# Finding and spreading the largest row sum of a weight block on VectorE alone, and moving two narrowed tiles of x into block 4

## The chip, the cores and the metric

The kernel runs on one core of a Trainium2 chip. The core has TensorE (matrix products, written to PSUM), VectorE, ScalarE and GpSimd (elementwise work and reductions), and SP, from whose queue most DMA transfers are issued. Each engine works off its own queue in order and waits for the others by semaphores. The metric is the time of one execution on the device in microseconds, as the median of several runs; smaller is better.

## The reference, cut to what matters

Attention with the heads mixed before and after the softmax gives x, of 1792 tokens (4 batches of 448) and 768 features; behind it stands a gated layer:

```python
rms = np.sqrt(np.mean(x * x, axis=-1, keepdims=True) + 1e-06)
xn = x / rms * rms_g
g = xn @ w_gate                      # 768 x 1536
silu = g * (1.0 / (1.0 + np.exp(-g)))
val = xn @ w_val                     # 768 x 1536
return (silu * val @ w_out).astype(np.float32)   # 1536 x 768
```

The weights come in as float64. The change touches only the gated layer, and there only the way in which weights and x are brought into float16.

## The kernel before, in words

The program has three stages. Attention runs first, to about 360 us of the span. Then come the gate and value products, and last the product with w_out, in which seven products take the place of eight.

**The gate and value products.** The 1536 columns of `w_gate` and `w_val` are cut into 12 blocks `f` of 128 columns. For each block and each batch `b` (0 to 3) `product` (L648) makes two results in PSUM, `pg` and `pv`, each a sum over six tiles `kk` of 128 features, and for each of these three matmuls of 448 columns: high part of the weights by high part of x, high by low, low by high (L652 to L654). That is 18 matmuls for `pg`, 18 for `pv`, 144 in a block. `swiglu` (L678) then makes silu(pg) times pv on ScalarE and VectorE and combines the results of several batches and blocks on GpSimd (L697). PSUM has six buffers for pg and pv, so TensorE can be three batches ahead of `swiglu`.

**Two kinds of blocks.** Blocks 0 to 3 (`PLAIN = 4`) hold weights and x as pairs of float32 values with a shortened mantissa. Blocks 4 to 11 hold both as pairs of float16 values, `wh`, `wl` and `xn`. For that the 24 tiles of x (4 batches by six features' tiles) are narrowed while blocks 1 to 3 are computed: `x_narrow` (L889) is called 1, 1, 3 and 3 times behind the four batches of each. One call scales a tile on VectorE (L900), rounds it on ScalarE (L901) and subtracts on VectorE or, for every third tile, on GpSimd (L902); `x_fetch` asks for the next tile on SP's queue.

**Weights.** `queue` and `queue_out` write a list of half blocks to be fetched and converted; `fetch` keeps two transfers ahead, `convert` takes at most one half for each batch. A conversion is ScalarE's L541, four VectorE instructions (L516 to L519) and, for a float16 block, ScalarE's L554, which sums the absolute values of each row into `half.sums`, one column for each half. From block 4 on the halves of `w_out` stand in the list as well (`if f >= PLAIN`, L955).

**The scale of a float16 block.** `even(f + 1, stage)` (L864) makes a power of two from the largest row sum of the block, so that the float16 values fit. `spread_max` (L562) does this with TensorE: a float32 matmul with the unit matrix brings the two columns of 128 sums into two rows (L564), VectorE takes their maxima (L568), a second float32 matmul with a matrix of ones spreads the sum of both to all 128 partitions (L572), and `power` (L579) makes the scale and its inverse with four VectorE instructions (L581 to L584). Each of the two matmuls is two passes on TensorE. Then ScalarE writes `wh` (L877) and VectorE `wl` (L878), both halves behind each other. `gain` (L849) does the same once, in block 0, for the vector `rms_g`.

**Order.** The order of all queues is the order in which the code is written. In blocks 3 to 10 `even` is called around the products of batch 2 (stage 0 between pg and pv, stage 1 behind pv) and of batch 3 (stage 2 ahead of pg, stage 3 behind pv), before `convert`, `x_narrow` and `swiglu` of that batch. So L564 stands in TensorE's queue between pg and pv of batch 2, and L572 behind pv of batch 2.

Of the kernel before, what the change touches and what calls it, by code (L numbers as in the profile page):

```python
# [7 lines left out]
F32 = mybir.dt.float32  # L8
# [32 lines left out]
PLAIN = 4  # L41
LEAST, MOST = 2.0 ** -90, 2.0 ** 100
# [5 lines left out]
def attention_moe(ctx: ExitStack, tc, q, k, v, wpre, wpost, mask, ident, wgv, wo, rms_g, out):  # L48
# [473 lines left out]
    def load_w(src, kind, pool_name=None, plain=None):  # L522
# [9 lines left out]
        def half(p):  # L532
# [11 lines left out]
            if kind == "wide":  # L544
                ks = slice(KT * p, KT * p + KT)
                hi, lo = pair
                f = c.bitcast(F32).rearrange("p (a f) -> p a f", f=128)
                nc.scalar.activation(hi[:, ks], f, AF.Copy)
                nc.gpsimd.tensor_tensor(lo[:, ks], f, hi[:, ks].bitcast(F32), ALU.subtract)
            elif kind == "narrow":  # L550
                half.plain.append(c.bitcast(F32))
                if not p:
                    half.sums = b_pools["tiny"].tile([128, 2], F32, name="wsum", tag="wsum", bufs=2)
                nc.scalar.activation(narrow(pair)[0][:, KT * p : KT * p + KT], half.plain[p].rearrange("p (a f) -> p a f", f=128), AF.Abs, scale=2.0 ** -12, accum_out=half.sums[:, p : p + 1])  # L554
# [7 lines left out]
    def spread_max(cols, many):  # L562
        ps = b_pools["ps0"].tile([128, S], F32, name="pst", tag="pv")
        nc.tensor.matmul(ps[:many, :128], cols, eye, start=True, stop=True)  # L564

        def top():
            m = b_pools["tiny"].tile([2, 1], F32, name="top", tag="top", bufs=2)
            nc.vector.tensor_reduce(m[:many], ps[:many, :128], AX.X, ALU.max)  # L568

            def back():  # L570
                o = b_pools["ps0"].tile([128, S], F32, name="pst", tag="pv")
                nc.tensor.matmul(o[:, :1], ones[:many], m[:many], start=True, stop=True)  # L572
                return o[:, :1]

            return back

        return top

    def power(v, up, more, name):  # L579
        t, p, s_, inv = (b_pools["tiny"].tile([128, 1], I32 if i in (1, 2) else F32, name=f"{name}{i}", tag=f"{name}{i}", bufs=2) for i in range(4))  # L580
        nc.vector.tensor_scalar(t, v, LEAST, MOST, ALU.max, ALU.min)  # L581
        nc.vector.tensor_scalar(p, t.bitcast(I32), 23, 23, ALU.logical_shift_right, ALU.logical_shift_left)
        nc.vector.tensor_scalar(s_, p, -1.0, float((254 + up) * 2 ** 23), ALU.mult, ALU.add)
        nc.vector.tensor_scalar(inv, p.bitcast(F32), 2.0 ** -up, more, ALU.mult, ALU.mult)  # L584
        return s_.bitcast(F32), inv
# [201 lines left out]
    def part_b(ps_p):  # L787
# [61 lines left out]
        def gain(stage, held={}):  # L849
            if stage == 0:  # L850
                held["sum"] = b_pools["tiny"].tile([128, 1], F32, name="gsum")
                held["g"] = b_pools["tiny"].tile([128, KT], F32, name="gabs")
                nc.scalar.activation(held["g"], g_sb, AF.Abs, accum_out=held["sum"])
            elif stage == 1:
                held["top"] = spread_max(held["sum"], 1)
            elif stage == 2:
                held["back"] = held["top"]()
            elif stage == 3:
                v = held["back"]()
                up, held["down"] = power(v, 8, 1.0, "gain")  # L860
                nc.vector.tensor_scalar(held["g"], g_sb, up, None, ALU.mult)
            return held

        def even(f, stage, held={}):  # L864
            if stage == 0:
                held["top"] = spread_max(halves[f].sums, 2)
            elif stage == 1:
                held["back"] = held["top"]()
            elif stage == 2:
                held["v"] = held["back"]()  # L870
            else:
                up, unit[f] = power(held["v"], 2, gain(4)["down"], "unit")
                hi, lo = w[f] = narrow(halves[f].pair)
                for p, c in enumerate(halves[f].plain):
                    ks = slice(KT * p, KT * p + KT)
                    c = c.rearrange("p (a f) -> p a f", f=128)
                    nc.scalar.activation(hi[:, ks], c, AF.Copy, scale=up)  # L877
                    nc.vector.scalar_tensor_tensor(lo[:, ks], c, up, hi[:, ks], ALU.mult, ALU.subtract)  # L878
# [10 lines left out]
        def x_narrow(many):  # L889
            for i in range(min(many, len(loaded))):  # L890
# [9 lines left out]
                nc.vector.scalar_tensor_tensor(raw, raw, gain(4)["g"][:, kk : kk + 1], ry_ps[0], ALU.mult, ALU.mult)  # L900
# [3 lines left out]
        def first_row():  # L904
# [27 lines left out]
            gain(2)  # L932
# [3 lines left out]
            gain(3)  # L936
# [16 lines left out]
        for f in range(1, FT - 1):  # L953
            queue(f + 1)
            if f >= PLAIN and outs:  # L955
                queue_out(outs.pop(0), f)
        for f in range(1, FT):
            plain = f < PLAIN
            for b in range(B):
# [9 lines left out]
                if even_next and b == 3:  # L969
                    even(f + 1, 2)  # L970
# [6 lines left out]
                if even_next and b == 3:  # L977
# [142 lines left out]
```

## Time and profile before

| What | us |
|---|---|
| three runs | 861.67, 861.85, 865.72 |
| median | 861.85 |
| profiled execution | 865.68 |
| its span, first to last instruction | 863.9 |
| TensorE busy in the span | 826.2 (96%) |
| VectorE, ScalarE, GpSimd busy | 600.8, 420.7, 361.8 |

The profile is of one execution. Its rows give the start of an instruction from the span's start, its duration, and in brackets how long the engine stood idle before it and what ended that. Successive matmuls overlap: what one costs is the distance between starts, not its duration. "PE" is TensorE, "DVE" VectorE, "ACT" ScalarE, "POOL" GpSimd. Block f begins with its first matmul `pg`: block 1 at 387.21, block 4 at 481.65, block 5 at 510.68.

### The profile page before, as it was taken

To read this page: it belongs to the slowest core of one execution; us is meant where nothing else is said; L and a number is where in the kernel's file an instruction comes from. 1 tells how busy PE (TensorE), PEld (TensorE's weight loads), DVE (VectorE), ACT (ScalarE), POOL (GpSimd) and SP (SyncE) were. 2 spreads that over 40 slices of the span, in tenths; PEclk is the share of its full clock that TensorE was granted. 3 is DMA by queue.
4 is the path that set the end of the run, shared out by engine and by line. 5 is a ranking of instruction groups with operands and counts; after the bars stand their busy time and mean duration, and the time that the engine had idled before them with its cause. 6 is when DMAs were issued, how large, how long until landed. Compare 5 with 4: busy or idle time off the path is not lost. (4 is left out here: it accounts for less than half of the span.)

```text
span 863.9 us, 26658 instructions
## 1 busy us (share of the span) xinstructions
PE 826.2 (96%) x10936; PEld 615.1 (71%) x10936; DVE 600.8 (70%) x1055; ACT 420.7 (49%) x931; POOL 361.8 (42%) x497
## 2 busy tenths in 40 slices
PE   7899989899999998999998999999999999999998
PEld 2668777677777776799997645555555569999997
DVE  5687776688777766877777776668656249976561
ACT  3677766577767766743333333233332235553310
POOL 7233445364645457944644411212112158572210
PEclk9999999999999999999999999999999999999999
DMA  7787768666756653752565365655554246664531
GB/s 213 195 229 214 219 189 234 189 193 208 224 180 189 203 161 117 222 197 80 186 197 158 103 204 168 180 183 151 167 150 166 75 137 189 184 194 139 169 131 64
DMA packets 81020, 150.06 MB, mean 174 GB/s; under 512 B 10767, under 2 KB 70317, under 8 KB 80899
## 3 DMA queue, kind: packets, MB, share of 16 engines
q1 hardware_dynamic: 76286, 134.72, 51.7%
q0 software_dynamic: 3648, 11.31, 4.9%
q10 hardware_dynamic: 965, 2.34, 0.8%
q8 instruction: 86, 1.41, 0.7%
q14 instruction: 35, 0.29, 0.1%
HBM read 77.55 MB, written 31.21 MB: 126 GB/s over the span
## 5 line engine op out<-in xcount | busy, mean ns | idle before, releaser
L184 PE MATMUL sp<-r,wk_pre 64*64 64x448 f32 x720 | 167.4, 554 | 4.7 <-DMA r<-st 3.4
L136 PE MATMUL qk<-k,q 64*64 64x448 f32 x768 | 157.7, 572 | 6.0 <-DMA q<-in_q 4.2
L198 ACT ACTIVATE e<-sp,nm 128x448 f32<-128x448 f32 x180 | 114.4, 639 | 91.8 <-DVE nm L191 90.1
L191 DVE TENSOR_REDUCE nm<-sp 128x1 f32<-128x448 f32 x180 | 111.5, 623 | 58.0 <-PE qk L136 26.7
L225 PEld LDWEIGHTS pm<-wn,e 60*64 60x64 f32 x5152 | 111.5, 136 | 48.2 <-POOL wn L210 22.6
L225 PE MATMUL pm<-wn,e 60*64 60x60 f32 x5152 | 110.0, 222 | 15.1 <-issue 11.1
L210 POOL TENSOR_SCALAR wn<-wk,rp 128x60 f32<-128x60 f32 x180 | 55.8, 322 | 163.4 <-DVE rp L207 146.4
L697 POOL TENSOR_TENSOR keep<-sg,keep 128x448 f32<-128x448 f32 x24 | 29.9, 1247 | 170.3 <-DVE sg L691 112.7
L269 PE MATMUL av<-at_all,v 64*64 64x240 f32 (+4 forms) x1728 | 94.4, 321 | 2.2 <-issue 2.2
L184 PEld LDWEIGHTS sp<-r,wk_pre 64*64 64x64 f32 x720 | 63.1, 136 | 21.3 <-ACT e L198 9.0
L136 PEld LDWEIGHTS qk<-k,q 64*64 64x64 f32 x768 | 56.0, 138 | 28.4 <-issue 8.3
L269 PEld LDWEIGHTS av<-at_all,v 64*64 64x64 f32 x1728 | 71.1, 134 | 4.4 <-issue 3.9
L652 PE MATMUL pg<-xn,wh 128*128 128x448 f16 x192 | 67.8, 353 | 0.0
L652 PE MATMUL pv<-xn,wh 128*128 128x448 f16 x192 | 67.8, 353 | 0.0
L654 PE MATMUL pg<-xn,wl 128*128 128x448 f16 x192 | 67.7, 353 | 0.0
L653 PE MATMUL pg<-xn,wh 128*128 128x448 f16 x192 | 67.7, 353 | 0.0
L653 PE MATMUL pv<-xn,wh 128*128 128x448 f16 x192 | 67.7, 353 | 0.0
L654 PE MATMUL pv<-xn,wl 128*128 128x448 f16 x192 | 67.7, 353 | 0.0
L238 DVE COPY at_all<-pm 128x420 f32<-128x420 f32 x92 | 54.4, 591 | 16.6 <-PE pm L225 16.3
L639 DVE TENSOR_TENSOR h<-hraw,h 128x448 fp32r<-128x448 f32 x54 | 61.4, 1182 | 3.9 <-ACT h L638 3.9
L825 POOL TENSOR_TENSOR fac<-wo,fac 128x768 fp32r<-128x768 f32 x21 | 41.4, 1989 | 53.6 <-ACT fac L824 53.6
L652 PEld LDWEIGHTS <-wh 128*128 128x128 f16 x384 | 37.5, 98 | 35.6 <-issue 1.8
(161 smaller groups left out, 1861.2 us busy)
## 6 DMA issues: line engine op xcount, KB each, us to landing
r<-st SPq DMA_DIRECT2D x117, 210.0 KB
hraw<-td SPq DMA_DIRECT2D x84, 224.0 KB
wraw<-in_wgv SPq DMA_DIRECT2D x20, 768.0 KB
td<-keep SPq DMA_DIRECT2D x48, 224.0 KB
wraw<-in_wo SPq DMA_DIRECT2D x12, 768.0 KB
r<-st SPq DMA_DIRECT2D x44, 175.0 KB
v<-in_v SPq DMA_DIRECT2D x24, 256.0 KB
q<-in_q POOLq DMA_DIRECT2D x28, 192.0 KB, 6.0
```

The lines of the kernel that those rows point to most:

```text
L136: nc.tensor.matmul(ps[j][m, :S], qt[n][sl, hp, m], kt[n // NC, hp][sl], start=True, stop=True)
L184: nc.tensor.matmul(o, wk_pre[sl], rt[n][sl, 2 * p + v_], start=True, stop=True)
L191: nc.vector.tensor_reduce(t, ps[:, :S], AX.X, ALU.max, negate=True)
L198: nc.scalar.activation(e, ps[:, :S], AF.Exp, bias=nmx.pop((n, p, u)), accum_out=sm[n, p][:, u : u + 1])
L210: nc.gpsimd.tensor_scalar(wn[n, p][:, u], wk, r[:, u : u + 1], 1.0, ALU.mult, ALU.mult)
L225: nc.tensor.matmul(o[:, :, at_], e[u_][sl, j : j + JT], w_, start=True, stop=True)
L238: nc.vector.tensor_copy(dst, src)
L269: nc.tensor.matmul(x, vt[b, hp][sl, j, c_], a, start=(c_ == 0), stop=(c_ == JC - 1))
L639: nc.vector.tensor_tensor(lo, raw, hi.bitcast(F32), ALU.subtract)
L652: nc.tensor.matmul(ps, a, xh[:, kk], start=(kk == 0), stop=False)
L653: nc.tensor.matmul(ps, a, xl_[:, kk], start=False, stop=False)
L654: nc.tensor.matmul(ps, a2, xh[:, kk], start=False, stop=(kk == KT - 1))
```

## The change

Three things change.

1. `spread_max` is gone. `largest` takes its place, on VectorE alone: two copies fold the 128 partitions of the sums into 32 (64 onto 64, 32 onto 32, side by side), a reduction leaves one value in each of 32 partitions, a 32x32 transpose puts these into one row, a second reduction gives the largest, a `tensor_scalar` bounds it and writes it 32 times into a row, and a second transpose spreads it to 32 partitions. `power` computes on 32 partitions and copies the two results to 64 and then to 128. The largest sum of any row and half is taken, no longer the sum of two maxima.
2. `even` is now called once for each half, in batches 2 and 3 of blocks 3 to 10, behind the products of the batch: the first call does all of the scale and the first half of `wh` and `wl`, the second call the second half. `gain` has two stages in place of four.
3. `AT_ONCE` sets the calls of `x_narrow`: block 3 does 1, 1, 2 and 2 and block 4 does 1 and 1. The halves of `w_out` stand in the list from block 5 on.

```diff
+AT_ONCE = {1: (1, 1, 3, 3), 2: (1, 1, 3, 3), 3: (1, 1, 2, 2), 4: (1, 1, 0, 0)}
...
-    def spread_max(cols, many):
-        ps = b_pools["ps0"].tile([128, S], F32, name="pst", tag="pv")
-        nc.tensor.matmul(ps[:many, :128], cols, eye, start=True, stop=True)
...
+    def largest(b, many):
+        if "square" not in b_pools:
+            b_pools["square"] = b_pools["tiny"].tile([32, 2, 32], F32, name="square")
+            nc.vector.memset(b_pools["square"], 0.0)
+        z = b_pools["square"]
+        nc.vector.tensor_copy(b[:64, many : 2 * many], b[64:, :many])
+        nc.vector.tensor_copy(b[:32, 2 * many : 4 * many], b[32:64, : 2 * many])
+        nc.vector.tensor_reduce(z[:, 0, :1], b[:32, : 4 * many], AX.X, ALU.max)
+        nc.vector.transpose(z[:, 1], z[:, 0])
+        nc.vector.tensor_reduce(b[:1, :1], z[:1, 1], AX.X, ALU.max)
+        nc.vector.tensor_scalar(z[:1, 1], b[:1, :1].to_broadcast([1, 32]), LEAST, MOST, ALU.max, ALU.min)
+        nc.vector.transpose(z[:, 0], z[:, 1])
+        return z[:, 0, :1]
+
+    def power(t, up, more, name):
+        o = b_pools["tiny"].tile([128, 3], F32, name=name, tag=name, bufs=2)
+        p, s_, inv = (o[:, i : i + 1] for i in range(3))
+        q = [x[:32].bitcast(I32) for x in (p, s_)]
+        nc.vector.tensor_scalar(q[0], t.bitcast(I32), 23, 23, ALU.logical_shift_right, ALU.logical_shift_left)
+        nc.vector.tensor_scalar(q[1], q[0], -1.0, float((254 + up) * 2 ** 23), ALU.mult, ALU.add)
+        nc.vector.tensor_scalar(inv[:32], p[:32], 2.0 ** -up, more[:32] if more is not None else 1.0, ALU.mult, ALU.mult)
+        nc.vector.tensor_copy(o[32:64, 1:], o[:32, 1:])
+        nc.vector.tensor_copy(o[64:, 1:], o[:64, 1:])
+        return s_, inv
...
-            elif stage == 3:
-                v = held["back"]()
-                up, held["down"] = power(v, 8, 1.0, "gain")
+                up, held["down"] = power(largest(held["sum"], 1), 8, None, "gain")
...
+        def even(f, p, held={}):
+            half = halves[f]
+            if not p:
+                held["up"], unit[f] = power(largest(half.sums, 2), 2, gain(2)["down"], "unit")
+                w[f] = narrow(half.pair)
+            up = held["up"]
+            hi, lo = (t[:, KT * p : KT * p + KT] for t in w[f])
+            c = half.plain[p].rearrange("p (a f) -> p a f", f=128)
+            nc.scalar.activation(hi, c, AF.Copy, scale=up)
+            nc.vector.scalar_tensor_tensor(lo, c, up, hi, ALU.mult, ALU.subtract)
...
-            if f >= PLAIN and outs:
+            if f > PLAIN and outs:
...
                 product(pg, (hi[:, :KT], lo[:, :KT]), x)
-                if even_next and b == 2:
-                    even(f + 1, 0)
                 product(pv, (hi[:, KT:], lo[:, KT:]), x)
-                if even_next and b == 2:
-                    even(f + 1, 1)
-                if even_next and b == 3:
-                    even(f + 1, 3)
+                if even_next and b >= 2:
+                    even(f + 1, b - 2)
                 convert(f)
-                if plain:
-                    for _ in range((1, 1, 3, 3)[b]):
-                        x_narrow(1)
-                        x_fetch(3)
+                for _ in range(AT_ONCE[f][b] if f <= PLAIN else 0):
+                    x_narrow(1)
+                    x_fetch(3)
```

VectorE's queue in block 3, batch 2 and the start of batch 3, before. `top` holds the two maxima, `xs` and `xn` are tiles of x, `g` and `u` belong to `swiglu`, `wl` is the low half of the next block's weights (both halves, x2):

```order
L568 TENSOR_REDUCE top<-pst 2x1
L900 SCALAR_TENSOR_TENSOR xs<-xs,gabs,psn 128x448
L902 TENSOR_TENSOR xn<-xs,xn 128x448
L900 SCALAR_TENSOR_TENSOR xs<-xs,gabs,psn 128x448 x2
L902 TENSOR_TENSOR xn<-xs,xn 128x448
L685 TENSOR_TENSOR g<-pg,ry_7899 128x448
L687 TENSOR_TENSOR u<-pv,ry_7899 128x448
L581 TENSOR_SCALAR unit_8891<-pst 128x1
L582 TENSOR_SCALAR unit_8892<-unit_8891 128x1
L583 TENSOR_SCALAR unit_8893<-unit_8892 128x1
L584 TENSOR_SCALAR unit_8894<-unit_8892,gain_8084 128x1
L878 SCALAR_TENSOR_TENSOR wl<-wc,unit_8893,wh 128x768 x2
```

The same place now:

```order
L568 COPY wsum<-wsum 64x2
L569 COPY wsum<-wsum 32x4
L570 TENSOR_REDUCE square<-wsum 32x1
L571 STREAM_TRANSPOSE square<-square 32x32
L572 TENSOR_REDUCE wsum<-square 1x1
L573 TENSOR_SCALAR square<-wsum 1x32
L574 STREAM_TRANSPOSE square<-square 32x32
L581 TENSOR_SCALAR unit<-square 32x1
L582 TENSOR_SCALAR unit<-unit 32x1
L583 TENSOR_SCALAR unit<-unit,gain 32x1
L584 COPY unit<-unit 32x2
L585 COPY unit<-unit 64x2
```

The scale's instructions stand in one piece, ahead of the first tile of x. Behind these twelve rows stands the first half of `wl`, then two tiles of x and the g and u of batch 2, and only then the second half.

TensorE's queue in block 4, from the end of pg to the start of pv of batch 2, before (with the loads of weights between the matmuls; `pst` is the PSUM tile of the sums):

```order
L653 MATMUL pg<-xn,wh 128x448
L654 LDWEIGHTS wl
L654 MATMUL pg<-xn,wl 128x448
L564 MATMUL pst<-eye,wsum 2x128
L652 LDWEIGHTS wh
L652 MATMUL pv<-xn,wh 128x448
L653 LDWEIGHTS wh
L653 MATMUL pv<-xn,wh 128x448
```

The same place now:

```order
L654 MATMUL pg<-xn,wh 128x448
L655 LDWEIGHTS wl
L655 MATMUL pg<-xn,wl 128x448
L653 LDWEIGHTS wh
L653 MATMUL pv<-xn,wh 128x448
L654 LDWEIGHTS wh
L654 MATMUL pv<-xn,wh 128x448
```

The matmul into `pst` is gone, and pv follows pg without anything between them.

## Rows read from the trace of the kernel before

**Rows 1.** Windows by stage: us, busy us (instructions) by engine, clock, DMA share, GB/s.

```profile
360.00:500.00 140.00, 134.99 (x659) 114.23 (x657) 105.15 (x151) 53.16 (x90) 67.21 (x56) 0.99 0.51 164
...
528.00:556.00 28.00, 28.00 (x150) 14.30 (x148) 20.02 (x27) 9.12 (x14) 6.46 (x5) 1.00 0.67 193
```

**Rows 2.** Timeline of TensorE, steady blocks: start, us, engine, line, op, tiles.

```profile
510.68 0.35 PE L652 MATMUL pg<-xn,wh 128*128 128x448 f16 x1
...
527.51 0.35 PE L654 MATMUL pg<-xn,wl 128*128 128x448 f16 x1
...
528.11 0.36 PE L652 MATMUL pv<-xn,wh 128*128 128x448 f16 x1
...
555.58 0.35 PE L654 MATMUL pg<-xn,wl 128*128 128x448 f16 x1
```

**Rows 3.** Timeline of TensorE, block 3 and the start of block 4.

```profile
464.77 0.37 PE L654 MATMUL pg<-x,wl 128*128 128x448 f32 x1
...
468.19 0.38 PE L564 MATMUL pst<-eye,wsum 128*2 128x128 f32 x2 [3.06 <-ACT wh L554]
...
469.88 0.57 PE L652 MATMUL pv<-x,wh 128*128 128x448 f32 x1
...
473.23 0.37 PE L652 MATMUL pv<-x,wh 128*128 128x448 f32 x1
...
474.55 0.37 PE L653 MATMUL pg<-x,wh 128*128 128x448 f32 x1
...
481.65 0.36 PE L652 MATMUL pg<-xn,wh 128*128 128x448 f16 x1
```

**Rows 4.** Timeline of TensorE, block 4, first pair.

```profile
499.72 0.38 PE L564 MATMUL pst<-eye,wsum 128*2 128x128 f32 x2 [0.88 <-ACT wh L554]
```

**Rows 5.** Timeline of VectorE, blocks 1, 3 and 4.

```profile
387.59 0.77 DVE L352 TENSOR_SCALAR i<-var 112x4 int32<-112x4 int32 x1
...
469.71 0.62 DVE L687 TENSOR_TENSOR u<-pv,ry 128x448 f32<-128x448 f32 x1
...
477.16 0.15 DVE L582 TENSOR_SCALAR unit<-unit 128x1 int32<-128x1 int32 x1
477.35 0.15 DVE L583 TENSOR_SCALAR unit<-unit 128x1 int32<-128x1 int32 x1
...
478.51 1.95 DVE L878 SCALAR_TENSOR_TENSOR wl<-wc,unit,wh 128x768 f16<-128x768 f32 x2 [0.88 <-ACT wh L877]
...
480.38 0.68 DVE L900 SCALAR_TENSOR_TENSOR xs<-xs,gabs,psn 128x448 f32<-128x448 f32 x1
...
481.69 0.62 DVE L902 TENSOR_TENSOR xn<-xs,xn 128x448 f16<-128x448 f32 x1 [0.64 <-ACT xn L901]
...
485.57 0.61 DVE L687 TENSOR_TENSOR u<-pv,ry 128x448 f32<-128x448 f32 x1
...
500.22 0.68 DVE L691 SCALAR_TENSOR_TENSOR sg<-pv,unit,sg 128x448 f32<-128x448 f32 x1 [1.52 <-ACT sg L690]
500.82 0.27 DVE L568 TENSOR_REDUCE top<-pst 2x1 f32<-2x128 f32 x1
```

**Rows 6.** Timeline of GpSimd, blocks 1 and 3.

```profile
387.15 1.18 POOL L688 TENSOR_TENSOR keep<-sg,u 128x448 f32<-128x448 f32 x1
...
470.55 1.14 POOL L688 TENSOR_TENSOR sg<-sg,u 128x448 f32<-128x448 f32 x1 [6.37 <-DVE top L568]
...
474.37 1.15 POOL L697 TENSOR_TENSOR u<-sg,keep 128x448 f32<-128x448 f32 x1
...
477.29 1.15 POOL L688 TENSOR_TENSOR sg<-sg,u 128x448 f32<-128x448 f32 x1 [0.38 <-ACT sg L686]
```

**Rows 7.** Timeline of ScalarE, block 3.

```profile
477.54 0.94 ACT L877 ACTIVATE wh<-wc,unit 128x768 f16<-128x768 f32 x1 [0.33 <-DVE unit L583]
```

**Rows 8.** Timeline of block 0: TensorE, then VectorE.

```profile
378.69 0.47 PE L644 MATMUL pg<-x,wh 128*128 128x448 f32 x1
...
373.96 2.66 DVE L622 SCALAR_TENSOR_TENSOR x<-raw,g_sb,x 128x448 fp32r<-128x448 f32 x4 [2.42 <-ACT x L621]
```

More of the change, by code (lines that the diff above doesn't have):

```diff
@@ L552, in half @@
                 if not p:
-                    half.sums = b_pools["tiny"].tile([128, 2], F32, name="wsum", tag="wsum", bufs=2)
+                    half.sums = b_pools["tiny"].tile([128, 8], F32, name="wsum", tag="wsum", bufs=2)
                 nc.scalar.activation(narrow(pair)[0][:, KT * p : KT * p + KT], half.plain[p].rearrange("p (a f) -> p a f", f=128), AF.Abs, scale=2.0 ** -12, accum_out=half.sums[:, p : p + 1])
@@ L560, in narrow @@
         return [t.rearrange("p a f -> p (a f)").bitcast(F16)[:, : FT * 128].rearrange("p (a f) -> p a f", f=128) for t in pair]
-    def spread_max(cols, many):
-        ps = b_pools["ps0"].tile([128, S], F32, name="pst", tag="pv")
-        nc.tensor.matmul(ps[:many, :128], cols, eye, start=True, stop=True)
[L566 to L585, printed above, removed]
+    def largest(b, many):
[11 more added lines that the diff above has]
+        return z[:, 0, :1]
@@ L850, in gain @@
             if stage == 0:
-                held["sum"] = b_pools["tiny"].tile([128, 1], F32, name="gsum")
+                held["sum"] = b_pools["tiny"].tile([128, 4], F32, name="gsum")
                 held["g"] = b_pools["tiny"].tile([128, KT], F32, name="gabs")
-                nc.scalar.activation(held["g"], g_sb, AF.Abs, accum_out=held["sum"])
+                nc.scalar.activation(held["g"], g_sb, AF.Abs, accum_out=held["sum"][:, :1])
             elif stage == 1:
-                held["top"] = spread_max(held["sum"], 1)
-            elif stage == 2:
-                held["back"] = held["top"]()
-            elif stage == 3:
-                v = held["back"]()
-                up, held["down"] = power(v, 8, 1.0, "gain")
+                up, held["down"] = power(largest(held["sum"], 1), 8, None, "gain")
                 nc.vector.tensor_scalar(held["g"], g_sb, up, None, ALU.mult)
             return held
[L864 to L878, printed above, removed]
+        def even(f, p, held={}):
[8 more added lines that the diff above has]
+            nc.vector.scalar_tensor_tensor(lo, c, up, hi, ALU.mult, ALU.subtract)
         ahead_x = [(b, kk) for b in range(B) for kk in range(KT)]
@@ L899, in x_narrow @@
                 hi, lo = (t[:, kk] for t in xn[b])
-                nc.vector.scalar_tensor_tensor(raw, raw, gain(4)["g"][:, kk : kk + 1], ry_ps[0], ALU.mult, ALU.mult)
+                nc.vector.scalar_tensor_tensor(raw, raw, gain(2)["g"][:, kk : kk + 1], ry_ps[0], ALU.mult, ALU.mult)
                 nc.scalar.activation(hi, raw, AF.Copy)
@@ L931, in first_row @@
             convert(0)
-            gain(2)
             for kk in range(KT):
@@ L935, in first_row @@
             swiglu(2, 0, *first_ps[2])
-            gain(3)
             last_rms(0)
@@ L968, in part_b @@
                 even_next = PLAIN - 1 <= f < FT - 1
-                if even_next and b == 3:
-                    even(f + 1, 2)
                 product(pg, (hi[:, :KT], lo[:, :KT]), x)
-                if even_next and b == 2:
-                    even(f + 1, 0)
                 product(pv, (hi[:, KT:], lo[:, KT:]), x)
-                if even_next and b == 2:
-                    even(f + 1, 1)
-                if even_next and b == 3:
-                    even(f + 1, 3)
+                if even_next and b >= 2:
+                    even(f + 1, b - 2)
                 convert(f)
-                if plain:
-                    for _ in range((1, 1, 3, 3)[b]):
-                        x_narrow(1)
-                        x_fetch(3)
+                for _ in range(AT_ONCE[f][b] if f <= PLAIN else 0):
+                    x_narrow(1)
+                    x_fetch(3)
                 swiglu(b, f, pg, pv)
```

## The prediction, made before the result was known

> **What bounds the kernel now.** I read the windows by stage first, then TensorE's timeline, then the other engines at the places where TensorE waits. In blocks 4 to 11 of the gated product TensorE is busy without a hole: 28.00 of 28 us, while VectorE is busy 20.02 [rows 1]. The stretch of 360 to 500 us, blocks 0 to 3, is the only one behind the attention part in which it loses time: 134.99 of 140. So time can be won by taking instructions out of TensorE's queue, and by taking waits out of that queue; an idle VectorE in the steady blocks costs nothing.
>
> What the spreading of the largest row sum costs TensorE shows in its starts. In a steady block the last matmul of pg starts at 527.51 and the first of pv at 528.11, 0.60 us instead of one pitch. A pitch is 0.1891 us: 89 of them lie between the first matmul of the block, 510.68, and 527.51. From 527.51 to the same place a block later, 555.58, are 28.07 us, and 144 pitches are 27.23 [rows 2]. So the two pairs of float32 matmuls (L564 and L572) cost 0.84 us in a block.
>
> In block 3 they cost more, because there TensorE stands in its queue before a sum that is not there yet: the pair at 468.19 waited 3.06 us for ScalarE's L554, and behind that wait the pitch goes from 0.203 to 0.37 us between 469.88 and 473.23, nine matmuls at the lower of the clock's two levels, 1.2 instead of 2.4 GHz, that lose 1.5 us [rows 3]. From 464.77 to 474.55 are 9.78 us for 20 pitches of 0.203 (35 of them lie between 474.55 and 481.65): 5.7 us lost in block 3 [rows 3]. In block 4 the pair waits again, 0.88 us [rows 4]; with the 0.84 of the pairs themselves that is 1.7 us. In block 0 the gain has two such pairs, for which I take the same 0.84, 0.8 us.
>
> **The change part by part.** *The matmuls leave.* Eight spreadings and one gain leave TensorE's queue. On TensorE this is 0.8 (block 0) + 5.7 (block 3) + 1.7 (block 4) + 6 x 0.84 = 5.0 (blocks 5 to 10) = 13.2 us, all on the path, as no other engine makes TensorE wait there.
>
> *What VectorE gets.* A chain of 12 small instructions takes the place of five (L568, L581 to L584). Nearest rows: L582 starts at 477.16 and L583, which reads its result, at 477.35, so 0.19 us a step; 12 steps are 2.3 us. For the 32x32 transposes and the copies between partitions the trace has no row; from below 0.15 (the duration of L582), from above 0.27 (the reduction L568 over 128 elements) [rows 5]: 1.8 to 3.2 us. I take 0.19, since the new rows have at most 32 elements. The Trainium skill (VectorE: DVE Perf Modes, The three transpose paths) gives 311 ns for a 128x128 bf16 transpose on VectorE; by it, as an estimate, the chain would be 0.24 us longer, and no run here shows one.
>
> There is one more price in the trace. L352, on 112x4 elements in SBUF, took 0.77 us from 387.59, and ended at 388.36, just as GpSimd's L688 did (387.15 + 1.18); without such a neighbour L582 takes 0.15 [rows 5, 6]. But L583, on 128x1, ran its 0.15 us at 477.35 beside GpSimd's L688 of 477.29 [rows 5, 6]. So some small instructions wait out a GpSimd instruction and some do not. The Trainium skill (SBUF — State Buffer, SBUF: two separate sides) says that the port pair that VectorE and GpSimd share is locked for a whole instruction; the row of L352 agrees, L583 shows that not every small one asks for it. By the rule alone the sum would be that of the late bound below.
>
> In block 3 the chain stands right behind u of b=1, which ends at 470.33 [rows 5], and there GpSimd runs four instructions without a pause, 470.55 to 475.52 [rows 6]. With no wait the chain ends at 472.6; with a wait for each of three of them at 475.5. I take 474.4, two waits.
>
> *What is late next.* Behind the chain ScalarE writes the first half of wh and VectorE the first half of wl, 0.95 us each (L877 0.94, L878 1.95 for two) [rows 5, 7]: ready at 476.3. TensorE, freed of 0.8 + 5.7, would begin block 4 at 475.15 instead of 481.65 [rows 3]; it begins at about 475.9, as two matmuls come before the first of wl. The second half stands behind two tiles of x (0.67 each for L900, and once 0.64 of waiting and 0.63 of L902: 2.6), g, ScalarE's sg and wh, and its own 0.97: 481.9. TensorE wants it 18 x 0.189 = 3.4 us into the block, at 479.3, and effectively gets it at 481.5. So VectorE takes back 3.0 us in block 4's first tile.
>
> *The narrowed x.* Two of the last six tiles leave block 3 for block 4, one each behind its two conversions, (3,4) and (3,5). VectorE ended block 3's u at 486.18 before [rows 5]; with four tiles in place of six, the longer chain and ScalarE's two separate turns I get 486.8. In block 4 h of b=1 started at 500.22 [rows 5]; with that 0.6 and the two tiles (0.7 and 1.9) it starts at 503.0 to 503.4. TensorE uses (3,5) at the end of pg of b=3, within half a microsecond of its being ready: 0.4 us, held in the next sum. Behind h comes the chain for block 5, 2.3 us and, with one wait for GpSimd, 3.4, then ScalarE and VectorE 0.95 each: about 507.9, so TensorE begins block 5 at 507.5. Before it began at 510.68 [rows 2]. Of 0.8 + 5.7 + 1.7 = 8.2 us only 3.2 are left here; VectorE takes 5.0. With no port waits it begins at 505.1 (5.6 left), with the most of them at 508.8 (1.9 left).
>
> *The conversions of w_out* go a block later, blocks 5 to 10 instead of 4 to 9. That empties VectorE's queue in the second half of block 4, so it catches up by block 5; block 10 becomes like the others, and before, it had no such conversions. Their next use is in block 11 and behind: hidden, cost zero. If the cover were gone, one conversion of about 4 us would stand before the first factors. The fetches on SP keep their distance of two.
>
> *The gain chain*, a memset and 13 steps, now stands in block 0 ahead of a conversion. At 0.19 it puts VectorE back by 2.7 us, and by 3.8 with one wait for GpSimd. TensorE reads the tiles behind it (x of batch 3) from 378.69 on, and VectorE split them from 373.96 on, 0.67 us each, where TensorE takes 1.2 for each [rows 8]: 4.7 us of cover, less the 0.4 by which TensorE is early. Cost zero; without the cover, up to 3.8 us. Four of the old five steps and L568 leave VectorE later in the block.
>
> *From block 5 on* VectorE has 20.02 less 0.9 (the five old instructions) plus 2.3 to 5.5 and 1.9 of waiting for ScalarE, 23.3 to 26.5 us in a block of 27.27. It fits, so all of the 5.0 us stays.
>
> **Sum.** 3.2 + 5.0 = 8.2 us, bounds 6.9 (1.9 + 5.0) and 10.6 (5.6 + 5.0). The profiled execution took 865.68 us (span 863.9) and would take 857.5. The median of the three runs is 861.85, 3.8 lower; the stretch in question is behind the attention part, and I take the saving as the same there: 853.7 us.
>
> **The rivals.** (a) No port waits: 10.6 us, 851.3. For it: the waits are inferred from one row. Against: GpSimd is at work exactly then. (b) The new hole in block 4 lets TensorE's clock fall again, as 3.06 us did in block 3: 1.5 us more, 855.2. For it: 2.2 us idle at once; against: the 0.88 us in block 4 did nothing, and 2.2 lies between [rows 3, 4]. (c) VectorE takes nothing back, as its instructions pack closer than I laid them: 13.2 us, 848.7. (d) The freed matmul time becomes a wait of the same size, so that the blocks keep 28.07 us: 3.2 left, 858.6. For it: VectorE's sum of 26.5 is near 27.27. (e) Slower: the 12 steps each pay what L352 paid, 0.77 us, 9.2 in all. Then a steady block needs 20.0 - 0.9 + 9.2 + 1.9 = 30.2 us against 28.07, 2.1 x 6 = 13 us more, and blocks 3 and 4, whose chain is then 9.2 instead of 3.3 to 4.1 us, lose about 2.3 instead of winning 3.2: about 877. It decides from a chain of 7.1 us on. Against: GpSimd has at most four instructions in a row there. (f) That the new chain does not spread the number to all partitions would show in the order; the two copies at its end reach all 128, so I give it nothing.
>
> **How the numbers follow.** Forecast 0.40, (a) 0.20, (b) 0.15, (c) 0.08, (d) 0.12, (e) 0.05. The likeliest is 853.7. The range goes from just above (c) to just beyond (d), 849.2 to 858.8. A difference of 0.5%, 4.3 us, is about what can be told from no change, so faster means under 857.5: forecast, (a), (b) and (c) hold 0.83, less 0.05 because one of three runs lay 3.9 us above the others: 0.78. The same: 0.17. Slower: 0.05.
>
> **What would show it.** Right: no float32 matmul between pg and pv, a period of 27.2 to 27.4 us in blocks 5 to 10, and in block 4 a wait of pv for wl of about 2 us that stands where the 3.06 us stood. Wrong: holes of TensorE in the steady blocks, transposes of over 0.5 us, a block 5 that begins less than 1.9 us earlier than before (then the chain was under-priced), or copies that run freely beside GpSimd (then it was over-priced).

## The result, and the profile after

The changed kernel takes 857.98 us (median of 20 runs, 854.41 to 865.09); the kernel before, run beside it, took 865.57 (20 runs, 861.67 to 870.97). The ratio is 0.9917 with a 95% interval of 0.9895 to 0.9939: about 7 us faster, 5.3 to 9.1 by the interval. The prediction was 8.2 us faster and 853.7 us. The absolute time is 4.3 us off mainly because the kernel before, in these runs, was 3.7 us above the 861.85 from which the prediction counted.

The profiled execution of the changed kernel took 861.31 us, with a span of 859.4. These are the two windows of [rows 1] in it.

```profile
360.00:500.00 140.00, 134.23 (x655) 113.41 (x654) 108.29 (x161) 51.22 (x88) 67.02 (x57) 0.99 0.49 153
528.00:556.00 28.00, 28.00 (x150) 14.48 (x149) 21.39 (x36) 9.14 (x14) 6.05 (x6) 1.00 0.63 185
```

In the steady window VectorE does 21.39 us where it did 20.02, and TensorE is still without a hole. Between 360 and 500 us TensorE is no fuller than it was, 134.23 against 134.99. So I looked for the gain in the steady blocks first, and TensorE's timeline says how much it is. It answers [rows 2]: the last matmul of a pg and the first of the next pv, and the first of block 7 and of block 8.

```profile
565.61 0.35 PE L653 MATMUL pg<-xn,wh 128*128 128x448 f16 x1
...
568.82 0.35 PE L655 MATMUL pg<-xn,wl 128*128 128x448 f16 x1
569.01 0.35 PE L653 MATMUL pv<-xn,wh 128*128 128x448 f16 x1
...
592.85 0.35 PE L653 MATMUL pg<-xn,wh 128*128 128x448 f16 x1
```

From 568.82 to 569.01 is one pitch, and from 565.61 to 592.85 are 27.24 us in place of 28.07. The float32 matmuls are gone, and each of blocks 6 to 10 has its 0.83 us back. The same stretch that [rows 3] shows, the end of block 3 and what follows, now reads so on TensorE:

```profile
478.89 0.55 PE L653 MATMUL pg<-xn,wh 128*128 128x448 f16 x1 [3.35 <-ACT wh L868]
...
479.94 0.56 PE L655 MATMUL pg<-xn,wl 128*128 128x448 f16 x1
...
482.16 0.41 PE L655 MATMUL pg<-xn,wl 128*128 128x448 f16 x1
482.40 0.35 PE L653 MATMUL pg<-xn,wh 128*128 128x448 f16 x1
...
486.02 0.36 PE L655 MATMUL pv<-xn,wl 128*128 128x448 f16 x1 [1.05 <-DVE wl L869]
...
510.44 0.36 PE L653 MATMUL pg<-xn,wh 128*128 128x448 f16 x1 [0.79 <-ACT wh L868]
...
511.49 0.36 PE L655 MATMUL pg<-xn,wl 128*128 128x448 f16 x1 [0.50 <-DVE wl L869]
```

The 3.06 us of waiting inside block 3 have become 3.35 us at the start of block 4, with 1.05 more at its first pv and 0.79 and 0.50 at the start of block 5. From 479.94 to 482.16 the pitch is 0.35 to 0.37 us, the lower of the clock's two levels, until it comes back to 0.19 at 482.40.

To compare executions I count from the first matmul of batch 1 in block 0, called the start of the stage here, since the attention part before it ends some us earlier or later in each execution. These are the first and the last matmul of it, before and then after:

```profile
363.52 0.72 PE L644 MATMUL pg<-x,wh 128*128 128x448 f32 x1
...
859.69 0.37 PE L654 MATMUL po<-h,fac 128*128 128x448 f32 x1
```

```profile
364.07 0.72 PE L645 MATMUL pg<-x,wh 128*128 128x448 f32 x1
...
855.22 0.37 PE L655 MATMUL po<-h,fac 128*128 128x448 f32 x1
```

From start to start the stage takes 496.17 and 491.15 us, 5.0 less. Block 5 starts 147.16 us into the stage before and 146.37 after. So blocks 0 to 4 brought 0.8 us where 3.2 were forecast, and the rest 4.2: six times 0.83, less the 0.7 us that block 5 still waits inside itself. That is the gap to explain. The medians differ by 7.6 us; the 2.6 beyond the stage's 5.0 lie outside the stage or in the scatter, and I don't explain them.

A stage time is that of one execution, and it scatters too. Up to block 5 the kernels `chain_x3` and `chain_x5` below are the changed kernel, instruction for instruction: block 5 starts 147.37 and 146.09 us into the stage there, against 146.37 here. So a difference of 1.3 us between two stages, or less, shows nothing by itself.

Next VectorE's row in block 3: u, the chain (L568 to L585) and the two halves of wl.

```profile
472.27 0.61 DVE L688 TENSOR_TENSOR u<-pv,ry 128x448 f32<-128x448 f32 x1
472.92 0.17 DVE L568 COPY wsum<-wsum 64x2 f32<-64x2 f32 x1
473.12 1.17 DVE L569 COPY wsum<-wsum 32x4 f32<-32x4 f32 x1
474.32 0.15 DVE L570 TENSOR_REDUCE square<-wsum 32x1 f32<-32x8 f32 x1
474.50 0.20 DVE L571 STREAM_TRANSPOSE square<-square 32x32 f32<-32x32 f32 x1
...
474.95 0.58 DVE L573 TENSOR_SCALAR square<-wsum 1x32 f32<-1x32 f32 x1
...
475.79 0.14 DVE L581 TENSOR_SCALAR unit<-square 32x1 int32<-32x1 int32 x1
...
476.26 0.45 DVE L584 COPY unit<-unit 32x2 f32<-32x2 f32 x1
476.75 1.05 DVE L585 COPY unit<-unit 64x2 f32<-64x2 f32 x1
478.87 1.02 DVE L869 SCALAR_TENSOR_TENSOR wl<-wc,unit,wh 128x768 f16<-128x768 f32 x1 [1.06 <-ACT wh L868]
...
484.40 1.57 DVE L869 SCALAR_TENSOR_TENSOR wl<-wc,unit,wh 128x768 f16<-128x768 f32 x1 [1.00 <-ACT wh L868]
```

And beside it GpSimd, the same four instructions as in [rows 6]:

```profile
473.11 1.16 POOL L689 TENSOR_TENSOR sg<-sg,u 128x448 f32<-128x448 f32 x1 [6.38 <-DVE wsum L568]
474.35 1.15 POOL L698 TENSOR_TENSOR keep<-sg,keep 128x448 f32<-128x448 f32 x1
475.57 1.13 POOL L698 TENSOR_TENSOR keep<-keep 128x448 f32<-128x448 f32 x1
476.66 1.13 POOL L698 TENSOR_TENSOR u<-sg,keep 128x448 f32<-128x448 f32 x1
```

The chain takes 4.9 us, 472.92 to 477.80. Its long rows end where a GpSimd row ends: L569 at 474.29 (GpSimd 474.27), L573 at 475.53 (475.50), L584 at 476.71 (476.70), L585 at 477.80 (477.79). Reductions, transposes and operations on one element a partition take 0.14 to 0.20 in the midst of it.

And in block 0, where the prediction gave the gain chain no cost:

```profile
368.43 0.15 DVE L568 COPY gsum<-gsum 64x1 f32<-64x1 f32 x1 [1.35 <-ACT gabs L854]
368.62 0.85 DVE L569 COPY gsum<-gsum 32x2 f32<-32x2 f32 x1
...
371.50 0.55 DVE L517 TENSOR_SCALAR wc<-wc 128x768 f32<-128x768 f32 x1
```

The same conversion before:

```profile
368.27 0.70 DVE L516 TENSOR_SCALAR wc<-wc 128x768 f32<-128x768 f32 x1 [2.16 <-ACT wc L541]
```

It starts 7.43 us into the stage now and started 4.75 us in before, so it is 2.7 us late, the forecast number. By u of batch 2 in block 0 2.0 us of that are left (23.56 us into the stage for 21.53). VectorE waits nowhere for TensorE between there and block 3, and these 2.0 stay: u of batch 1 in block 3 stands at 108.20 and stood at 106.19 [rows 5].

### The profile page after: what moved, and what is told of

Read it like the earlier page. It is cut to its first block, busy times and chain, and to the rows that moved or that the text cites. A ratio compares the mean times of both kernels' runs of the same rounds, so it can differ in the third digit from the quotient of the medians.

```text
span 859.4 us, 26654 instructions
## 1 busy us (share of the span) xinstructions
PE 814.8 (95%) x10900; PEld 608.2 (71%) x10900; DVE 615.8 (72%) x1119; ACT 422.0 (49%) x931; POOL 360.3 (42%) x497
## 3 DMA queue, kind: packets, MB, share of 16 engines
q8 instruction: 86, 1.41, 0.7%
## 5 line engine op out<-in xcount | busy, mean ns | idle before, releaser
L185 PE MATMUL sp<-r,wk_pre 64*64 64x448 f32 x720 | 162.2, 540 | 5.2 <-DMA r<-st 1.8
L137 PE MATMUL qk<-k,q 64*64 64x448 f32 x768 | 153.3, 556 | 6.3 <-DMA q<-in_q 4.1
L655 PEld LDWEIGHTS <-wl 128*128 128x128 f16 x384 | 37.7, 98 | 38.4 <-DVE wl L869 3.3
```

Of the source, the lines that this page charges most:

```text
L137: nc.tensor.matmul(ps[j][m, :S], qt[n][sl, hp, m], kt[n // NC, hp][sl], start=True, stop=True)
L185: nc.tensor.matmul(o, wk_pre[sl], rt[n][sl, 2 * p + v_], start=True, stop=True)
L655: nc.tensor.matmul(ps, a2, xh[:, kk], start=False, stop=(kk == KT - 1))
```

## The experiments

Two theories stood against each other. **A**: VectorE's row of work from block 0 to the chain for block 5 sets when TensorE can go on in blocks 4 and 5, and the gain was lost there, 2.0 us by the gain chain and the rest by copies that wait out GpSimd. **B**: the loss sits on TensorE itself, in a clock that falls behind a wait or in waits that the moved tiles or conversions bring.

### The two halves of the change

`x_and_wo_only` is the kernel before with only the new places of x and w_out:

```diff
+AT_ONCE = {1: (1, 1, 3, 3), 2: (1, 1, 3, 3), 3: (1, 1, 2, 2), 4: (1, 1, 0, 0)}
...
-            if f >= PLAIN and outs:
+            if f > PLAIN and outs:
...
-                    for _ in range((1, 1, 3, 3)[b]):
+                for _ in range(AT_ONCE[f][b] if f <= PLAIN else 0):
```

> The kernel before with the moved tiles of x and the later w_out conversions alone; the sums still go through TensorE. My theory (the gain is TensorE's float32 matmuls and the wait in front of them): L564 still waits about 3 us in block 3, since the two conversions ahead of its sum are unmoved, the steady period stays 28.07 us, and the time is within 2 us of before. Rival (the moved tiles bring the gain, by emptying VectorE in block 3): 4 to 7 us faster than before, with a block 3 of under 33 us.

Measured: 864.31 us, ratio 0.9988 (0.9956 to 1.002); the stage takes 496.86 us, and the period, the time from one steady block to the next, is 28.07. The waits of TensorE between 400 and 690 us (what waited, for what: us in all, times, longest) are now one, where there were two:

```profile
PE pst L565 <- ACT wh L555: 3.6, 1, 3.6
```

`spread_only` is the other half, the new chain with the old places:

```diff
-AT_ONCE = {1: (1, 1, 3, 3), 2: (1, 1, 3, 3), 3: (1, 1, 2, 2), 4: (1, 1, 0, 0)}
+AT_ONCE = {1: (1, 1, 3, 3), 2: (1, 1, 3, 3), 3: (1, 1, 3, 3), 4: (0, 0, 0, 0)}
...
-            if f > PLAIN and outs:
+            if f >= PLAIN and outs:
```

> The changed kernel with x and w_out as before; only the sums are on VectorE. My theory: the steady period is 27.24 us all the same, and VectorE, with one more tile of x (1.3 to 1.9 us) ahead of the second half of wl in block 3 and conversions of w_out right behind the chain in block 4, delays blocks 4 and 5: 1 to 3 us slower than the changed kernel, still 3 to 6 us faster than before. Rival (the moved tiles bring the gain): as slow as before.

Measured: 860.78 us, ratio 0.9965 (0.9937 to 0.9992); the stage takes 494.12 us, period 27.24. So the steady blocks win their 0.83 us by the chain alone, and the moved tiles and conversions bring nothing alone but 3.0 us (494.12 to 491.15) once the chain stands on VectorE: the tile takes work out of the row in front of block 4's second half of wl. What the tiles bring and what the conversions was not run apart. The waits of pv in block 4 were 1.79 and 0.65 us here, and the clock fell a second time.

### What makes VectorE late

`gain_by_tensor` is the changed kernel with the gain's largest sum found as before, by two float32 matmuls, a reduction and four small steps:

```diff
-                up, held["down"] = power(largest(held["sum"], 1), 8, None, "gain")
+                nc.tensor.matmul(ps[:1, :128], held["sum"][:, :1], eye, start=True, stop=True)
...
+                nc.tensor.matmul(o[:, :1], ones[:1], held["top"][:1], start=True, stop=True)
```

> The changed kernel, but the gain of block 0 still goes through TensorE; the eight scales of the blocks are on VectorE. Theory A (the gain chain put VectorE back by 2.7 us in block 0, and 2.0 of it stayed until block 3, because VectorE waits for nothing of TensorE in between): u of batch 1 in block 3 comes 2.0 us earlier against the start of the stage, TensorE waits 1.3 instead of 3.35 us at the start of block 4, its clock does not fall behind it (1.5 us more), and the time is 2 to 3 us shorter than the changed kernel's, the 0.8 us of the two pairs already taken off. Theory B (VectorE was late in this one profile by chance): the wait in block 4 stays between 2 and 3.5 us and the time is 0.8 us longer than the changed kernel's.

Measured: 857.39 us, ratio 0.9927 (0.9896 to 0.9958). u of batch 1 in block 3 (u of block 3, from here on) stands 106.55 us into the stage, so 1.6 of the 2.0 us of delay are gone. That is more than the scatter: the four executions with the gain's chain of copies on VectorE have it at 107.90 to 109.22 (`chain_x5` 107.90, `spread_only` 108.09, 108.20 after the change, `chain_x3` 109.22), the three with the gain on TensorE (before, `x_and_wo_only` and this one) at 106.19 to 106.69. Block 4 starts after a wait of 0.44 us instead of 3.35; 1.3 of the difference is that TensorE comes later itself, with its float32 pairs of block 0 back (block 3 starts 83.02 us into the stage instead of 81.72). The clock doesn't fall, and the stage takes 489.49 us, 1.7 less than after the change. The times of whole runs can't tell 1.7 us.

`reduce_copies` leaves the chain where it is, but its four copies and the broadcast become reductions over an axis of one element, which compute the same:

```diff
+    def copy(o, x):
+        nc.vector.tensor_reduce(o, x.unsqueeze(2), AX.X, ALU.max)
...
-        nc.vector.tensor_copy(b[:64, many : 2 * many], b[64:, :many])
+        copy(b[:64, many : 2 * many], b[64:, :many])
...
-        nc.vector.tensor_scalar(z[:1, 1], b[:1, :1].to_broadcast([1, 32]), LEAST, MOST, ALU.max, ALU.min)
+        nc.vector.tensor_scalar(b[:1, 1:2], b[:1, :1], LEAST, MOST, ALU.max, ALU.min)
+        copy(z[:1, 1], b[:1, 1:2].to_broadcast([1, 32]))
...
```

> The changed kernel, but the four small copies and the instruction that writes the bounded maximum 32 times are reductions over an axis of one element, which the profile never showed waiting for GpSimd; one small instruction more. Theory A (the copies wait out GpSimd's instructions): the chain of block 3 takes 2.4 to 2.7 us instead of 4.9, whatever GpSimd does, TensorE waits about 1 us instead of 3.35 at the start of block 4, and the time is 2.4 to 4 us shorter than the changed kernel's (the larger if the clock does not fall). Theory B (the long copies are slow for another reason, their crossing of partitions): the chain stays at 4 to 5 us and the time is the changed kernel's.

Measured: 854.43 us, ratio 0.9896 (0.9854 to 0.9939), and the stage takes 487.02 us, 4.1 less than after the change. VectorE's row in block 3 (two copies, the broadcast, two copies), then GpSimd's beside it:

```profile
469.89 0.33 DVE L564 TENSOR_REDUCE wsum<-wsum 64x2 f32<-64x2 f32 x2
...
471.05 0.17 DVE L564 TENSOR_REDUCE square<-wsum 1x32 f32<-1x32 f32 x1
...
471.96 0.33 DVE L564 TENSOR_REDUCE unit<-unit 32x2 f32<-32x2 f32 x2
```

```profile
470.08 1.15 POOL L693 TENSOR_TENSOR sg<-sg,u 128x448 f32<-128x448 f32 x1 [6.38 <-DVE wsum L564]
471.30 1.15 POOL L702 TENSOR_TENSOR keep<-sg,keep 128x448 f32<-128x448 f32 x1
```

Thirteen instructions take 2.4 us in the midst of the same GpSimd work, 0.33 for each pair of former copies, where one copy took up to 1.17. The data and the engine are the same, the kind of instruction is another: so it was the kind that waited. The Trainium skill (SBUF — State Buffer, SBUF: two separate sides) says more than the prediction quoted: VectorE asks for the port pair that it shares with GpSimd in a perf mode that uses two ports, or with two inputs from SBUF. These rows agree with that as far as they go: copies and a tensor_scalar over several elements waited, reductions didn't. In which mode an instruction ran no row shows.

### Do the two delays add up, and what is left

`both_mends` has both edits.

> The changed kernel with both mends at once: the gain's largest sum by TensorE as before the change, and the chain's four copies and its broadcast as reductions over an axis of one element. By theory A (the gain chain made VectorE late in block 0; the copies wait out GpSimd's instructions) the two losses lie one behind the other on VectorE, so u of the second tile of block 3 comes 106.0 to 106.6 us behind the stage's first matmul (gain by TensorE alone 106.55, reductions alone 107.20) and the chain takes 2.4 us; but TensorE pays about 0.8 again in block 0. The stage lasts about 486.9 us (reductions alone 487.02). Rival B: the two mend the same delay, since with reductions the gain chain has no waits left to lose; then u comes at 107.2 and the stage is 0.8 us longer than with the reductions alone, 487.8.

Measured: 854.74 us, ratio 0.9882 (0.9844 to 0.9920); u of block 3 at 106.23 us, the stage 485.99. That is where theory A has u, and the stage is 1.8 us under rival B's 487.8. Against the reductions alone it is 1.0 us, which two executions of one program can differ by, so that the two delays add up is likely and not shown by the stage alone. What TensorE still waits between 400 and 690 us:

```profile
PE pv L659 <- DVE wl L890: 1.1, 1, 1.1
PE pg L659 <- DVE wl L890: 0.5, 1, 0.5
```

`early_half` starts from `reduce_copies` and asks whether the waits of pv in block 4 are a loss of their own:

```diff
-                    even(f + 1, b - 2)
+                    if f > PLAIN:
+                        even(f + 1, b - 2)
+                    elif b == 2:
+                        even(f + 1, 0)
+                        even(f + 1, 1)
```

> The kernel with reductions in place of the copies, and in blocks 3 and 4 both halves of the next block's weights are made right behind the chain, the second no longer behind the tiles of x of the tile between. With reductions alone pv of block 4 still waits 1.27 us for wh and 1.04 for wl, and pg of block 5 0.25 and 0.50. Theory C: what VectorE has to do between the chain of block 3 and the chain of block 4 sets when block 5 can begin, so the 2.3 us that pv no longer waits come back as a longer wait at the start of block 5 (3.0 us in place of 0.75), and the stage stays within 0.5 us of 487.0. Rival D: the waits of pv are a loss of their own; then they go, block 5 still waits 0.75, and the stage lasts 484.7 us, 2.3 less.

Measured: 854.11 us, ratio 0.9869 (0.9819 to 0.9919); the stage takes 487.84 us, 0.8 longer than with the reductions alone. The waits of TensorE between 400 and 690 us:

```profile
PE pg L657 <- ACT xn L896: 1.6, 1, 1.6
...
PE pg L658 <- DVE xn L897: 0.3, 1, 0.3
```

The waits of pv are gone, and 1.6 and 0.3 us stand elsewhere, at the last tile of x in block 4 (I expected them at the start of block 5, which waits no more). VectorE begins the first wl for block 5 at 142.38 us into the stage, and with the reductions alone at 142.28, so its row ends where it ended: order within it doesn't help. That block 5 still starts at 143.81 instead of 142.30 is TensorE's clock, which fell behind these waits; nine matmuls like these lose about 1.6 us:

```profile
499.78 0.58 PE L657 MATMUL pv<-xn,wh 128*128 128x448 f16 x1
...
502.76 0.48 PE L659 MATMUL pv<-xn,wl 128*128 128x448 f16 x1
```

So the 0.8 us say nothing against theory C. They are within the scatter besides.

`late_lo_both` makes the row shorter. It starts from `both_mends`; the subtraction that makes the low part of a tile of x is written behind the next tile's first step or behind g and u, instead of waiting there for ScalarE's high part, and the next tile is fetched as much later:

```diff
+        def late():
+            while pend:
+                nc.vector.tensor_tensor(*pend.pop(), ALU.subtract)
...
-                (nc.gpsimd if kk % 3 == 1 else nc.vector).tensor_tensor(lo, raw, hi, ALU.subtract)
+                late()
+                if kk % 3 == 1:
+                    nc.gpsimd.tensor_tensor(lo, raw, hi, ALU.subtract)
+                else:
+                    pend.append((lo, raw, hi))
...
                 swiglu(b, f, pg, pv)
+                late()
```

> Both mends, and VectorE no longer stands still between the two halves of narrowing a tile of x: the subtraction that makes the low part, which waited 0.64 to 0.88 us for ScalarE's high part, is written behind the next tile's first step, or behind g and u where there is none. Theory C: VectorE's row of work from block 1 to the chain of block 4 sets what TensorE still waits in blocks 4 and 5 (with both mends 1.05 us at pv of block 4 and about 0.9 at the start of block 5). 16 tiles go that way, so VectorE is 5 to 10 us less behind; u of the second tile of block 3, 106.2 us behind the stage's first matmul, comes at 97 to 101, no wait is left in blocks 4 and 5, and the stage lasts about 484.1 us, 1.9 less. Rival: the loads of x, of which one is now asked for a step later, or ScalarE's order set that place, and the stage stays at 485.7 to 486.3.

Measured: u of block 3 at 98.9 us, and between 400 and 690 us TensorE waits for nothing at all; the stage takes 483.96 us. That is 12.2 us less than before the change, of the 13.2 that the prediction takes off TensorE; the gain's pairs, which stay on TensorE here, keep the other 1.0, so nothing of note is lost any more. The whole runs take 856.15 us, ratio 0.9886 (0.9833 to 0.9938), which is not less than the 854.74 of `both_mends`: their scatter is wider than the 2.0 us, and the saving shows only in the stage of one execution.

| kernel | stage, us | TensorE waits, 400 to 690 us |
|---|---|---|
| before | 496.17 | 3.9 |
| x_and_wo_only | 496.86 | 3.6 |
| spread_only | 494.12 | 7.1 |
| after | 491.15 | 5.8 |
| gain_by_tensor | 489.49 | 4.5 |
| early_half | 487.84 | 2.9 |
| reduce_copies | 487.02 | 3.4 |
| both_mends | 485.99 | 1.6 |
| late_lo_both | 483.96 | 0.0 |

So theory A holds: what shortens VectorE's row takes waits off TensorE, until none is left. Of B, the moved tiles and conversions bring no wait of their own (`x_and_wo_only`), and the clock's fall after the change cost nothing, as the rows of block 4 show (see rival (b) below).

### How much more the steady blocks could carry

`chain_x3` and `chain_x5` are the changed kernel with the chain three and five times in a row for the scales of blocks 6 to 11, which are made in blocks 5 to 10; the first results are not used. The edit of `chain_x3` (`chain_x5` has `range(4` in it):

```diff
+                for _ in range(2 if f > 5 else 0):
+                    power(largest(half.sums, 2), 2, gain(2)["down"], "spare")
                 held["up"], unit[f] = power(largest(half.sums, 2), 2, gain(2)["down"], "unit")
```

> The changed kernel, but for blocks 6 to 10 the chain of 12 instructions stands three times in a row (the first two results are not used). A repeat takes 2.3 us without waits and 3.75 with those that the first one had, so the chain grows from 3.75 to between 8.4 and 11.3 us. Theory: in a steady block the first half of wl is ready 7.2 us before TensorE wants it, and VectorE is busy 20.6 of 27.24; with two repeats of about 2.6 both nearly fit: period 27.24 to 27.8. Rival (e) of the prediction, every step at 0.77 us or a limit of 7.1 us of chain: period 28.4 or more.

> As before it, with the chain five times in a row for blocks 6 to 10: four repeats of about 2.6 us, 10.4 more. Theory: VectorE then has 20.6 + 10.4 and 1.9 of waiting for ScalarE, 32.9 us, in a block of 27.24, and becomes the bound: TensorE waits at the start of each such block, and the period is 30 to 33 us; five periods are 14 to 28 us longer. Rival: VectorE's other work moves into the holes it had and the chain is still hidden: 27.24 to 28.

Measured, one run each: 882.32 and 910.32 us. A repeat takes 2.29 us (L568 of one repeat starts at 656.09, of the next at 658.38). With two repeats, blocks 7 to 10 take 30.67, 31.77, 30.66 and 32.02 us, on average 31.28; with four, blocks 6 to 10 take 35.24 to 36.60, on average 35.98. The theory for `chain_x3` fell, and it came out at rival (e)'s end; that for `chain_x5` had the bound right and the size too small (30 to 33 us). What VectorE waits for after the change says why, first in block 6 (538.37 to 565.61), then in block 7 (565.61 to 592.85):

```profile
DVE keep L692 <- ACT sg L691: 1.6, 1, 1.6
DVE sg L692 <- ACT sg L691: 1.5, 1, 1.5
DVE wc L517 <- ACT wc L542: 1.5, 1, 1.5
DVE wl L869 <- ACT wh L868: 1.1, 1, 1.1
```

```profile
DVE sg L692 <- PE pv L655: 2.5, 1, 2.5
DVE sg L692 <- ACT sg L691: 1.6, 1, 1.6
DVE wl L869 <- ACT wh L868: 1.1, 1, 1.1
DVE wc L517 <- ACT wc L542: 0.6, 1, 0.6
```

VectorE is idle for 6.6 us in either block (these waits and the short gaps between instructions), but in block 6 it waits for ScalarE alone, which in turn waited for what VectorE had made late (`wc`, with `sg` of `swiglu` in the queue behind it) and once for the load of a weight. Only in every second block does it wait for TensorE, 2.5 us, and more than half of that is covered. This is the row of ScalarE that makes the same sg, and VectorE's row:

```profile
577.84 0.61 ACT L691 ACTIVATE sg<-pg,unit 128x448 f32<-128x448 f32 x1
```

```profile
579.50 0.68 DVE L692 SCALAR_TENSOR_TENSOR sg<-pv,unit,sg 128x448 f32<-128x448 f32 x1 [2.54 <-PE pv L655]
```

ScalarE ends at 578.45; without TensorE VectorE would have waited until then, and TensorE costs it the 1.05 us from there to 579.50, in two blocks. With two repeats it doesn't wait for TensorE even there:

```profile
DVE sg L692 <- ACT sg L691: 3.1, 2, 1.6
DVE wl L871 <- ACT wh L870: 2.1, 2, 1.1
...
```

Those are VectorE's waits in `chain_x3` from 631.08 to 661.74. So the waits for ScalarE belong to VectorE's own row, and its time to spare is small. The runs give it twice: 4.58 us more work made a block 4.04 longer, and 9.16 made it 8.74 longer. About 0.5 us a block were to spare, which is the 1.05 in two blocks; not the 7.2 by which the first half of wl is ready early, and not the 6.6 of idle time.

## Why the prediction was right or wrong

- **The number: right, in part by luck.** 8.2 us were forecast, the medians fell by 7.6, and 853.7 and 857.98 us differ mostly by the kernel before. But the stage that the sum is about gave 5.0, and 0.8 of the 3.2 us forecast for blocks 0 to 4. That block 5 would begin less than 1.9 us earlier was named as a sign that the chain was under-priced, and it came.
- **The freed matmuls: right.** 0.84 us a steady block were forecast and 0.83 came in each of blocks 6 to 10; block 5 kept 0.7 of its share back in the wait at its start. That the block has one stream of matmuls without holes [rows 2] made this term safe. The gain's pairs, taken at the same 0.84, gave a little more: block 1 starts 22.68 us into the stage for 23.69, block 3 81.72 for 83.02.
- **The gain chain at zero: wrong, and this is the step that failed.** The cover, 4.7 us until TensorE reads batch 3, is real but the wrong one: it says that TensorE doesn't wait in block 0, not that VectorE ever catches up. VectorE had no wait for TensorE up to block 3, so 2.0 us arrived there, where it is late already. `gain_by_tensor` takes 1.6 of them away. The delay of 2.7 us behind the chain came as forecast, but by luck: the chain first waited 1.35 us for its sum and then 0.7 for GpSimd, which that number holds nothing of, and the conversion behind it had stood 2.16 us waiting for ScalarE before, which the number doesn't take off.
- **The chain in block 3: the mechanism right, the size short.** Small instructions do wait out GpSimd; two waits were taken and four came, 4.9 us in place of 4.1. `reduce_copies` shows both, with 2.4 us for the chain without them; 2.3 had been worked out. With the 2.0 of the gain chain and 0.2 of ScalarE and VectorE behind it, the first half of wl is ready 3.0 us later into the stage than forecast (115.8 for 112.8). Block 4 starts 2.4 later (114.8 for 112.4), as its first matmul needs wh alone.
- **Block 5: a slip in the sum, and the delay.** From h at 503.0 to 503.4, with its own 0.6, the chain's 3.4 and 0.95 each for ScalarE and VectorE, wl would be ready at 508.9 to 509.3, not at the 507.9 that stands there: 1.0 to 1.4 us. So 2 us and not 3.2 would have been left by the prediction's own rows. Measured, block 5 starts 146.4 us into the stage and not 144.0. Of these 2.4 us, that slip makes about half; the other half is h, which comes 1.6 to 2.0 us late (141.5 for 139.5 to 139.9), less the 0.3 by which the chain there was shorter (3.1 us) and the 0.4 by which TensorE began earlier ahead of wl.
- **The tiles of x and w_out: right as far as shown.** Moving both costs nothing that shows, and together they are worth 3.0 us, but only with the chain on VectorE; the two were not run apart.
- **Rival (b), the clock: it happened and cost nothing.** The clock fell behind the 3.35 us, and the seven matmuls from 479.94 to 482.40 lost 1.1 us. But pv then waited until 486.02 for a wl that VectorE ended at 485.97: TensorE would have stood that much longer. A loss on TensorE counts only where TensorE is the bound, and there VectorE was. In `early_half`, where no wait stood behind it, the same fall did cost.
- **The steady blocks: right in the result, with a margin that I had mis-sized.** A row of 23.3 to 26.5 us was worked out for a block of 27.27; the repeats show one of about 26.7, since the waits for ScalarE are 3.3 to 5.7 us and not the 1.9 that I added. Rival (e), decided from a chain of 7.1 us, was nearer than its chance of 0.05 says: with 0.5 us to spare behind chains of 3.1 and 3.75 in turn, a block grows from a chain of about 4 us on and is as long as before, 28.07, from about 4.8.
- **Rivals (a), (c), (d): not what came.** There were port waits, VectorE took time back, and the period did fall. The reductions, which take the port waits away, give 9.15 us (496.17 less 487.02) of the 10.6 of (a).

## What to carry to other kernels

A delay on an engine that is not the bound is free only if that engine waits for the bound somewhere behind it; follow its row to the next such wait, and add up what arrives there. What it can take on without harm is at most that wait, and only the part of it that no third engine covers (here 1.05 of 2.5 us), not its idle time: waits for third engines that work for it belong to its own row. And where VectorE works beside GpSimd, count small copies at what a GpSimd instruction takes (here 1.13 to 1.16 us), or write them as a reduction over an axis of one element.

## What the runs showed of the hardware

- Beside a GpSimd instruction float32 copies of 32x4, 32x2 and 64x2 took up to 1.17, 0.85 and 1.08 us and a tensor_scalar over 1x32 up to 0.58 (the 1.08 in `gain_by_tensor`), and without one 0.15 to 0.17. The same moves as reductions took 0.14 to 0.18 at any time.
- A 32x32 float32 transpose on VectorE took 0.199 to 0.202 us in every run, beside GpSimd or not.
- Waits of TensorE of 1.41 and 0.50 us, close together at the start of a block, were followed by 3.0 us at the lower clock in `chain_x3` (pitch 0.37 from 601.42 to 604.40 us); 1.19 and 0.50 in the block before were not. In `early_half` 1.62 and 0.31 were. What decides between them stays open.
